# Another order of the first steps, and of attention's steps in the later batches, in a fused block attention and gated MLP kernel

## The chip, the cores and the metric

The kernel runs on one core of a Trainium2 chip. The metric is the device time of one launch in microseconds. The engines of the core work side by side, each through its own queue in order: TensorE (PE, matmuls), VectorE (DVE), ScalarE (ACT), GpSimd (POOL), and SyncE (SP), whose queue issues all DMAs here.

## What is computed

Eight batches of 576 tokens go through block attention (8 heads of 64, chunks of 64 tokens that attend only to themselves), and its result x through a gated MLP with a residual:

```python
scores = scale * np.matmul(q_c, k_c.transpose(0, 1, 2, 4, 3))       # per chunk and head, 64 x 64
attn = softmax(scores);  x = attn @ v_c                             # x: 8 x 576 x 512
h = gelu_tanh(x @ w_in)                                             # 512 -> 1024
u, v = h[..., :512], h[..., 512:]
v_n = (v - mean(v)) / np.sqrt(var(v) + 1e-06) * g_ln                # over the 512 columns
v_s = np.einsum('ts,bsd->btd', w_sg, v_n) + b_sg[None, :, None]     # mixes the 576 tokens
out = x + (u * v_s) @ w_out
```

All is float32. Matmuls split each operand into a high and a low part and add three products.

## The kernel before

**Attention** goes by 36 tiles of 128 rows (two chunks, all heads); a batch has 4.5. A tile takes three steps. `S` (att_scores): 16 matmuls of 64x64 into PSUM (from tile 5 on at L393), then softmax: maximum and subtraction on DVE (L404, L417), exp on ACT (L420), sum and reciprocal on DVE (L426 to L428), division on POOL (L429; on DVE up to tile 8). `T` (att_transpose): from tile 5 on a block transpose on DVE (L443), a copy on ACT (L446), two small copies on ACT (L451) and two on DVE (L453). `O` (att_out): 16 matmuls (L481) into a PSUM buffer, which ACT and DVE empty into xh, xl and xf, the high part, the low part and the whole of x (L101, L104, L503).

**The MLP** of a batch goes by units. `v0` to `v4` (v_unit, 12 matmuls of 512 columns, L523): gelu on ACT (L526), statistics on DVE, a power on POOL, normalization on DVE and ACT. An even batch has five (the fifth holds the odd 64 tokens of two batches, L545 to L547), an odd one four. `u0` to `u3` (24 matmuls of 288 columns, L560): gelu (L567). `s0` to `s3` (token mixing, 28 matmuls, L580): the product with u on DVE (L585), more sums, and its split into gh and gl. Then the output: batches 0 and 1 in four units `o` (24 matmuls, L700); later batches in seven products `p1 p5 p2 p6 p3 p7 p4` (12 matmuls each, L647) of quarter matrices, whose sums of w_out are formed once (`B`, ten POOL adds, L265), split (`C`, split_sum, L278) and kept in DRAM. `p4` runs after the next batch's v0 (the name `last`).

**Buffers** that tie steps together: three PSUM buffers `pm` for all units and for `O` (a unit waits until the one three before it has been emptied), one pair of banks for scores, 3 softmax tiles `pt`, 2 transposed tiles `ptT`.

**The order.** START is a hand-written list for the beginning: w_in's loads and conversion (L, W, w for the v half, X, x for the u half), attention's steps (A loads, S, T, O, and P and Q for S and O of two tiles), w_sg's split (G, g), w_out's conversion (Y), fill matmuls (D), and the units with batch and number (`s12` is s2 of batch 1). It ends within batch 2. From there a loop goes through the units of each batch in program order, and SLOTS says after which unit attention's steps for the coming tiles are recorded: the line 1 for odd batches, 0 for even ones, digits counting tiles from the first of that even batch or, in an odd batch, of the next even one. A step at p7 of an even batch comes only after the next batch's v0 (the list `later`). A scheduler orders what has been recorded; from batch 2 on PE's matmuls keep the written order, while DVE, ACT and POOL may take other orders.

Of the kernel before, what the change touches and what calls it, by code (L numbers as in the profile page):

```python
# [42 lines left out]


START = """
L0 A0 L1 A1 L2 L3 A4 W0 S0 W1 D8 w0 S1 W2 T0 w1 S2 O0 T1 W3 w2 S3 O1 T2 M0 w3 S4 O2 T3 v00 X0 O3 G0 T4 v01 x0 X1 O4 A8
v02 x1 X2 v03 X3 v04 u00 x2 g0 g1 u01 x3 g2 P5 g3 u02 g4 T5 u03 T6 s00 P7 Q5 s01 s02 T7 T8 s03 v10 Q7 v11 Y0 v12 Y1
v13 Y2 u10 Y3 u11 Y4 u12 Y5 Y6 u13 Y7 A10 s10 A12 s11 P9 s12 s13 T9 o00 B0 T10 P11 o01 B1 o02 B2 o03 Q9 B3 A14 T11 o10
B4 T12 o11 Q11 S13 A15 C5 B5 o12 B6 T13 o13 P14 A17 C6 B7 v20 B8 v21 O13 C7 B9 v22 K0
"""  # L50

PE_TILES = 5
# [5 lines left out]


SLOTS = {  # L60
    1: "v0:T0 v1:T1 u0:O01 u0:S23 u2:T2 u3:T3 s0:O23 s0:S4 p2:T4 p7:S56",
    0: "v0:O4 v3:T5 u0:T6 u1:O56 u1:S78 u3:T7 s0:T8 p7:O78 p7:S9A",
}


# [754 lines left out]
```

## Time and profile before

| | us |
|---|---|
| median of three runs (518.04 to 520.42) | 518.08 |
| the profiled execution, its own time | 519.43 |
| its span | 517.5 |
| PE busy in it | 491.1 |
| DVE, ACT, POOL busy | 385.6, 288.9, 90.8 |

A matmul's end in the trace is modelled, so that PE looks busy also where matmuls stand far apart. What a stage loses is read from the distance between the starts of its units, against the same units in a stretch without waits. TensorE's granted clock is 1.00 (2.4 GHz) almost everywhere and 0.50 (1.2 GHz) in two short stretches.

### The profile page before, as it was taken

The page shows a single profiled execution, that of the slowest core. Times are in us where ns is not written, and L with a number is a line of the kernel's source. Part 1 is how long each engine was busy: PE and PEld are TensorE (multiplying, and loading weights), DVE is VectorE, ACT ScalarE, POOL GpSimd, SP SyncE. Part 2 cuts the span into 40 slices and gives each one's busy share as a digit, 9 for nine tenths or more (in the row PEclk, how much of TensorE's full clock was granted, in tenths as well). Part 3 has the DMA queues.
Part 4 walks back from the last instruction along what each step waited for, and adds up shares of the span by engine and source line. Part 5 has one row for each costly group of instructions (what it writes and reads, how often), then busy time and mean ns, then how long its engine had stood idle before and what let it go on. Part 6 is the DMA issues. An engine that isn't in the chain of part 4 may idle for free.

```text
span 517.5 us, 12516 instructions
## 1 busy us (share of the span) xinstructions
PE 491.1 (95%) x5172; PEld 451.6 (87%) x5172; DVE 385.6 (75%) x783; ACT 288.9 (56%) x533; POOL 90.8 (18%) x94
## 2 busy tenths in 40 slices
PE   5999999999988969999999999999999999999996
PEld 4667898799987759997999889997899889998996
DVE  7998779988877856567869786667869786666165
ACT  5898767744264657217763678417763678414220
POOL 0112100202323601102120221102120221102000
PEclk9999999999999888999999999999999999999999
DMA  8857010245175784097444804087444910082006
GB/s 328 324 163 198 1 42 15 91 122 145 70 227 170 218 292 85 4 311 187 124 122 138 275 27 124 4 305 191 124 123 138 265 38 1 3 297 78 0 10 204
DMA packets 61356, 72.28 MB, mean 140 GB/s; under 512 B 36082, under 2 KB 47858, under 8 KB 61300
## 3 DMA queue, kind: packets, MB, share of 16 engines
q1 hardware_dynamic: 61300, 71.49, 45.1%
q8 instruction: 40, 0.66, 0.5%
q14 instruction: 16, 0.13, 0.1%
HBM read 58.36 MB, written 13.11 MB: 138 GB/s over the span
## 4 chain that ended last, share of the span: by engine, by line
PE 62%; DVE 20%; ACT 10%; POOL 2%; issue 2%; DMA 2%; SPq 0%; ACTq 0%; DVEq 0%; POOLq 0%
PE pm L580 17%; PE pm L560 14%; PE pm L523 14%; PE pm L647 9%; PE pm L700 3%; DVE xl L104 2%; PE banks L393 2%; DVE gl L104 2%; PE pm L185 1%; DVE sm L529 1%; DVE ptT L453 1%; DVE pt L417 1%; PE pm L481 1%; DVE v L541 1%; DVE den L426 1%
## 5 line engine op out<-in xcount | busy, mean ns | idle before, releaser
L580 PE MATMUL pm<-wsg,v 128*128 128x288 f32 x768 | 108.0, 297 | 0.5 <-ACT u L567 0.5
L580 PEld LDWEIGHTS pm<-wsg,v 128*128 128x128 f32 x768 | 103.9, 189 | 1.3 <-ACT u L567 1.0
L532 POOL TENSOR_TENSOR sm<-sm,neg_half 128x1 f32<-128x1 f32 x36 | 36.4, 1012 | 167.6 <-DVE sm L531 164.1
L523 PE MATMUL pm<-win_h,xl 128*128 128x512 f32 x128 | 52.3, 409 | 4.5 <-ACT hs L526 2.5
L560 PE MATMUL pm<-xh,win_l 128*128 128x288 f32 x256 | 56.3, 301 | 0.0
L429 POOL TENSOR_TENSOR pt<-pt,den 128x512 f32<-128x512 f32 x27 | 28.4, 1063 | 155.2 <-DVE den L428 134.3
L560 PE MATMUL pm<-xl,win_h 128*128 128x288 f32 x256 | 55.6, 299 | 0.0
L560 PE MATMUL pm<-xh,win_h 128*128 128x288 f32 x256 | 55.5, 298 | 0.0
L523 PE MATMUL pm<-win_l,xh 128*128 128x512 f32 x128 | 51.6, 403 | 0.0
L523 PE MATMUL pm<-win_h,xh 128*128 128x512 f32 x128 | 51.4, 401 | 0.0
L101 ACT CAST gh<-u 128x576 fp32r<-128x576 f32 x24 | 16.2, 675 | 50.5 <-DVE u L585 26.7
L560 PEld LDWEIGHTS pm<-xh,win_l 128*128 128x128 f32 x256 | 41.9, 191 | 1.3
L560 PEld LDWEIGHTS pm<-xh,win_h 128*128 128x128 f32 x256 | 41.6, 191 | 0.0
L560 PEld LDWEIGHTS pm<-xl,win_h 128*128 128x128 f32 x256 | 41.6, 191 | 0.0
L647 PE MATMUL pm<-gh,ring 128*128 128x288 f32 x192 | 40.1, 295 | 0.0
L540 ACT ACTIVATE v<-hs,sm 128x512 fp32r<-128x512 f32 x32 | 23.2, 725 | 24.6 <-POOL sm L532 24.6
L526 ACT ACTIVATE hs<-pm 128x512 f32<-128x512 f32 x36 | 21.1, 595 | 25.7 <-PE pm L523 25.4
L529 DVE BATCH_NORM_STATS2 sm<-hs 128x6 f32<-128x512 f32 x36 | 24.4, 684 | 14.1 <-ACT hs L526 14.1
L523 PEld LDWEIGHTS pm<-win_h,xl 128*128 128x128 f32 x128 | 24.4, 191 | 11.8 <-ACT hs L526 2.9
L647 PE MATMUL pm<-tv,ring 128*128 128x288 f32 x216 | 32.4, 299 | 1.8 <-ACT ptT L446 1.2
L541 DVE SCALAR_TENSOR_TENSOR v<-hs,sm,v 128x512 fp32r<-128x512 f32 x32 | 24.4, 762 | 11.3 <-ACT v L540 11.1
L104 DVE TENSOR_TENSOR gl<-u,gh 128x576 fp32r<-128x576 f32 x24 | 18.4, 765 | 18.9 <-ACT gh L101 18.9
(146 smaller groups left out, 1049.6 us busy)
## 6 DMA issues: line engine op xcount, KB each, us to landing
ring<-factors SPq DMA_DIRECT2D x42, 512.0 KB, 4.9
qkv_t<-qkv SPq DMA_DIRECT2D x32, 512.0 KB, 4.9
qkv_t<-qkv SPq DMA_DIRECT2D x124, 64.0 KB, 4.0
out_dram<-u SPq DMA_DIRECT2D x18, 288.0 KB, 4.9
out_dram<-ot SPq DMA_DIRECT2D x14, 288.0 KB, 3.7
qkv_t<-qkv SPq DMA_DIRECT2D x3, 768.0 KB, 11.8
wsg<-w_in SPq DMA_DIRECT2D x4, 512.0 KB, 6.2
wout<-w_in SPq DMA_DIRECT2D x4, 512.0 KB, 8.5
```

Source lines behind the costliest of these rows:

```text
L101: nc.scalar.copy(hi, src)
L104: lo_eng.tensor_tensor(lo, src, hi.bitcast(F32), op=ALU.subtract)
L429: (nc.gpsimd if t > last[1] else pick(f"n{t}")).tensor_tensor(pt, pt, den.unsqueeze(2).broadcast_to([P, H, D]), op=ALU.mult)
L523: pin(nc.tensor.matmul(pv, a[:, kt, tok], c[:, kt, DH:], start=(i == 0), stop=(i == 11)))
L526: nc.scalar.activation(h, pv, AF.Gelu_apprx_tanh, scale=-1.0)
L529: nc.vector.bn_stats(st, h)
L532: nc.gpsimd.tensor_tensor(rs, rs, neg_half, op=ALU.pow)
L540: nc.scalar.mul(hi, h, rs)
L541: nc.vector.scalar_tensor_tensor(lo, h, rs, hi.bitcast(F32), op0=ALU.mult, op1=ALU.subtract)
L560: pin(nc.tensor.matmul(pm[:, j, :HS], a[:, kt, dc], c[:, kt, j * HS : (j + 1) * HS], start=(i == 0), stop=(i == 11)))
L580: pin(nc.tensor.matmul(pm[:, j, :HS], a[:, dc], c[:, m, j * HS : (j + 1) * HS], start=(i == 0), stop=(i == len(ops) - 1)))
L647: pin(nc.tensor.matmul(pm[:, e, :HS], a[:, k, e * P : (e + 1) * P], c[:, k, :], start=starts and i == 0, stop=i == len(ops) - 1, skip_grou ...
```

## The change

Two tables of step names are replaced; no function changes, and every unit, tile and instruction form stays. Of START the first line and, below it, the part from batch 1's mixing units on (the conversion of w_out, Y, also moves ahead of more of batch 1's units, and v04 behind u00); SLOTS whole:

```diff
-L0 A0 L1 A1 L2 L3 A4 W0 S0 W1 D8 w0 S1 W2 T0 w1 S2 O0 T1 W3 w2 S3 O1 T2 M0 w3 S4 O2 T3 v00 X0 O3 G0 T4 v01 x0 X1 O4 A8
+L0 A0 L1 A1 L2 S0 D6 L3 W0 A4 W1 w0 S1 W2 w1 T0 S2 O0 T1 w2 W3 O1 T2 M0 w3 S3 O2 S4
...
-v13 Y2 u10 Y3 u11 Y4 u12 Y5 Y6 u13 Y7 A10 s10 A12 s11 P9 s12 s13 T9 o00 B0 T10 P11 o01 B1 o02 B2 o03 Q9 B3 A14 T11 o10
-B4 T12 o11 Q11 S13 A15 C5 B5 o12 B6 T13 o13 P14 A17 C6 B7 v20 B8 v21 O13 C7 B9 v22 K0
+s10 o00 A10 P9 A12 T9 s11 A14 s12 T10 s13 B0 P11 o01 B1 o02 B2 T11 B3 Q9 o03 A15 o10 B4 T12 B5 C5 o11
+B6 S13 Q11 o12 T13 B7 C6 o13 B8 A17 v20 O13 B9 C7 P14 v21 v22 K0
...
 SLOTS = {
-    1: "v0:T0 v1:T1 u0:O01 u0:S23 u2:T2 u3:T3 s0:O23 s0:S4 p2:T4 p7:S56",
-    0: "v0:O4 v3:T5 u0:T6 u1:O56 u1:S78 u3:T7 s0:T8 p7:O78 p7:S9A",
+    1: "v1:T1 v2:T0 u0:O01 u0:S23 u3:T3 u3:T2 s0:S4 s0:O23 p3:S56 p7:T4",
+    0: "v0:O4 u0:T6 u1:S78 u2:T5 s1:O56 s2:T8 s3:T7 p3:O78 p3:S9A",
 }
```

The line numbers of the kernel after are higher by one. Three places in the order of the engines' queues:

**ACT, batch 2, from the end of its v units into its u units**, before (`z` belongs to v4, `fac` is the split of a w_out sum, `u` the gelu of u0 and u1, `ptT` the transposes of tile 15, the next four rows empty the output of tiles 14 and 15):

```order
181 L545 ACTIVATE z_0_94<-hs,sm 64x512
182 L545 ACTIVATE z_1_95<-hs,sm 64x512
183 L546 CAST z_0_96<-z_0_94 64x512
184 L546 CAST z_1_97<-z_1_95 64x512
185 L277 CAST fac<-sums 128x512
186 L567 ACTIVATE u_2407<-pm 128x576 x2
187 L446 COPY ptT<-blocks 128x512
188 L451 COPY ptT<-blocks 32x8x32 x2
189 L101 CAST xh<-pm 128x2x4x64
190 L503 COPY xf<-pm 128x2x4x64
191 L101 CAST xh<-pm 128x2x4x64
192 L503 COPY xf<-pm 128x2x4x64
```

and after, the same stretch:

```order
187 L546 ACTIVATE z_0_94<-hs,sm 64x512
188 L546 ACTIVATE z_1_95<-hs,sm 64x512
189 L547 CAST z_0_96<-z_0_94 64x512
190 L547 CAST z_1_97<-z_1_95 64x512
191 L278 CAST fac<-sums 128x512
192 L568 ACTIVATE u_2397<-pm 128x576 x2
193 L447 COPY ptT<-blocks 128x512 x2
194 L452 COPY ptT<-blocks 32x8x32 x3
195 L421 ACT_TABLE_LOAD
196 L421 ACTIVATE pt<-pt 128x512 x2
197 L568 ACT_TABLE_LOAD
198 L568 ACTIVATE u_2397<-pm 128x576
```

Before, the output of tiles 14 and 15 (its emptying starts with `xh`) follows tile 15's copies directly; now the copies of both tiles are followed by the softmax of tiles 16 and 17 and the gelu of u2, and the emptying begins seven rows behind the last row shown. Ahead of the stretch, the exps of tiles 14 and 15 stood together before v20's gelu, with one table load behind them; now they stand apart among the gelus of v21 to v24, with four table loads.

**ACT, the first v units of batch 3**, before (`hs` is a gelu of a v unit, L420 the exp of tiles 18 and 19, L446 and L451 their transposes):

```order
206 L540 ACTIVATE v<-hs,sm 128x512
207 L420 ACT_TABLE_LOAD
208 L420 ACTIVATE pt<-pt 128x512 x2
209 L526 ACT_TABLE_LOAD
210 L526 ACTIVATE hs<-pm 128x512
211 L446 COPY ptT<-blocks 128x512 x2
212 L451 COPY ptT<-blocks 32x8x32 x4
213 L540 ACTIVATE v<-hs,sm 128x512
214 L526 ACTIVATE hs<-pm 128x512 x2
```

and after:

```order
218 L421 ACT_TABLE_LOAD
219 L421 ACTIVATE pt<-pt 128x512 x2
220 L527 ACT_TABLE_LOAD
221 L527 ACTIVATE hs<-pm 128x512
222 L541 ACTIVATE v<-hs,sm 128x512
223 L527 ACTIVATE hs<-pm 128x512
224 L447 COPY ptT<-blocks 128x512
225 L452 COPY ptT<-blocks 32x8x32 x2
226 L527 ACTIVATE hs<-pm 128x512
227 L541 ACTIVATE v<-hs,sm 128x512
228 L447 COPY ptT<-blocks 128x512
229 L452 COPY ptT<-blocks 32x8x32 x2
```

The exp now comes ahead of v0's gelu, and each tile's copies stand a v unit further back, between gelus.

**DVE, the products of batch 3**, before (`kept`, `ot` and `u` by L653 empty the products, `tv` is the split for p7 and p4, L443 the block transpose of tile 22):

```order
414 L653 TENSOR_TENSOR kept<-pm,xf 128x576
415 L653 TENSOR_TENSOR ot<-pm,kept 128x576
416 L104 TENSOR_TENSOR tv<-u_3104,tv 128x576
417 L443 STREAM_TRANSPOSE blocks<-pt 128x512
418 L653 TENSOR_TENSOR u_3104<-pm,xf 128x2x288
419 L453 COPY ptT<-blocks 32x8x32 x2
420 L653 TENSOR_TENSOR u_3104<-pm,u_3104 128x2x288
```

and after:

```order
419 L654 TENSOR_TENSOR kept<-pm,xf 128x576
420 L654 TENSOR_TENSOR ot<-pm,kept 128x576
421 L105 TENSOR_TENSOR tv<-u_3102,tv 128x576
422 L654 TENSOR_TENSOR u_3102<-pm,xf 128x2x288
423 L444 STREAM_TRANSPOSE blocks<-pt 128x512
424 L654 TENSOR_TENSOR u_3102<-pm,u_3102 128x2x288
425 L454 COPY ptT<-blocks 32x8x32 x2
```

The block transpose has gone from ahead of p6's sum (`u<-pm,xf`) to behind it.

## Rows read from the trace of the kernel before

**Rows 1.** Page, parts 1 and 6: busy us and share; a load's KB, us to landing.

```profile
PE 491.1 (95%) x5172; PEld 451.6 (87%) x5172; DVE 385.6 (75%) x783; ACT 288.9 (56%) x533; POOL 90.8 (18%) x94
...
qkv_t<-qkv SPq DMA_DIRECT2D x32, 512.0 KB, 4.9
```

**Rows 2.** Stages: us, busy PE, PEld, DVE, ACT, POOL (count), clock, DMA share, GB/s.

```profile
0.00:66.90 66.90, 59.53 (x616) 46.07 (x617) 57.97 (x124) 52.27 (x127) 9.91 (x14) 1.00 0.60 196
66.90:145.35 78.45, 77.54 (x874) 73.60 (x873) 66.66 (x153) 43.95 (x85) 15.81 (x13) 1.00 0.31 90
145.35:202.14 56.79, 47.90 (x550) 43.03 (x549) 41.02 (x81) 32.84 (x58) 16.15 (x16) 0.91 0.71 212
...
226.62:286.00 59.38, 57.13 (x694) 53.22 (x692) 44.84 (x90) 35.26 (x58) 10.31 (x11) 1.00 0.57 168
286.00:343.11 57.11, 57.11 (x578) 53.74 (x577) 43.06 (x86) 33.66 (x55) 10.54 (x11) 1.00 0.40 123
```

**Rows 3.** Chain that ended last: start us, us, engine, tile, line, matmul passes.

```profile
194.45 7.86 PE pm L560 x48
...
292.58 11.20 PE pm L523 x48
303.78 6.40 PE pm L560 x48
310.18 1.09 PE pm L481 x64
...
318.79 14.91 PE pm L580 x112
333.71 9.56 PE pm L647 x72
```

**Rows 4.** PE's timeline, 145 to 203 us: start us, us, line, [idle before <-releaser].

```profile
149.16 0.79 PE L481 MATMUL pm<-ptT,qkv_t 64*64 64x64 f32 x32 [0.45 <-ACT xf L503]
150.91 1.05 PE L481 MATMUL pm<-ptT,qkv_t 64*64 64x64 f32 x29 [0.96 <-ACT ptT L451]
...
169.06 0.50 PE L523 MATMUL pm<-win_h,xl 128*128 128x512 f32 x1 [2.48 <-ACT hs L526]
...
191.19 1.44 PE L481 MATMUL pm<-ptT,qkv_t 64*64 64x64 f32 x29 [4.90 <-ACT ptT L451]
```

**Rows 5.** The two stretches at the lower clock (the ninth field).

```profile
169.95:173.35 3.40, 3.40 (x10) 2.62 (x9) 3.40 (x9) 2.34 (x6) 3.27 (x4) 0.50 1.04 290
...
190.45:197.25 6.80, 6.06 (x108) 5.80 (x109) 3.23 (x7) 3.98 (x8) 0.00 (x0) 0.50 1.02 272
```

**Rows 6.** ACT's timeline, 184 to 200 us.

```profile
184.83 1.47 ACT L545 ACTIVATE z<-hs,sm 64x512 fp32r<-64x512 f32 x2 [2.32 <-POOL sm L532]
...
190.74 0.83 ACT L451 COPY ptT<-blocks 32x256 f32<-32x256 f32 x2
...
196.57 1.28 ACT L420 ACT_TABLE_LOAD   x1
197.87 1.38 ACT L420 ACTIVATE pt<-pt 128x512 f32<-128x512 f32 x2
```

**Rows 7.** PE's timeline in batch 3: two rows with a wait.

```profile
246.53 1.16 PE L481 MATMUL pm<-ptT,qkv_t 64*64 64x64 f32 x64 [1.35 <-ACT hs L526]
...
284.25 1.82 PE L647 MATMUL pm<-tv,ring 128*128 128x288 f32 x12 [0.62 <-ACT ptT L446]
```

**Rows 8.** DVE's timeline ahead of these two waits.

```profile
240.53 0.71 DVE L443 STREAM_TRANSPOSE blocks<-pt 128x512 f32<-128x512 f32 x1 [1.09 <-POOL pt L429]
...
282.81 0.70 DVE L443 STREAM_TRANSPOSE blocks<-pt 128x512 f32<-128x512 f32 x1
```

**Rows 9.** DVE's and POOL's timelines, 142 to 152 us.

```profile
143.19 2.44 DVE L453 COPY ptT<-blocks 32x256 f32<-32x256 f32 x2 [0.74 <-ACT ptT L446]
...
150.46 0.60 DVE L453 COPY ptT<-blocks 32x256 f32<-32x256 f32 x2 [0.68 <-ACT ptT L446]
...
142.83 2.66 POOL L265 TENSOR_TENSOR sums<-sums,wout 128x512 f32<-128x512 f32 x2
```

More of the change, by code (lines that the diff above doesn't have):

```diff
@@ L45 @@
 START = """
-L0 A0 L1 A1 L2 L3 A4 W0 S0 W1 D8 w0 S1 W2 T0 w1 S2 O0 T1 W3 w2 S3 O1 T2 M0 w3 S4 O2 T3 v00 X0 O3 G0 T4 v01 x0 X1 O4 A8
-v02 x1 X2 v03 X3 v04 u00 x2 g0 g1 u01 x3 g2 P5 g3 u02 g4 T5 u03 T6 s00 P7 Q5 s01 s02 T7 T8 s03 v10 Q7 v11 Y0 v12 Y1
-v13 Y2 u10 Y3 u11 Y4 u12 Y5 Y6 u13 Y7 A10 s10 A12 s11 P9 s12 s13 T9 o00 B0 T10 P11 o01 B1 o02 B2 o03 Q9 B3 A14 T11 o10
-B4 T12 o11 Q11 S13 A15 C5 B5 o12 B6 T13 o13 P14 A17 C6 B7 v20 B8 v21 O13 C7 B9 v22 K0
+L0 A0 L1 A1 L2 S0 D6 L3 W0 A4 W1 w0 S1 W2 w1 T0 S2 O0 T1 w2 W3 O1 T2 M0 w3 S3 O2 S4
+T3 X0 v00 O3 T4 x0 X1 v01 X2 v02 O4 x1 x2 A8 X3 v03 G0 u00 g0 g1 P5 x3 T5 g2 v04 u01 g3 u02
+g4 u03 T6 s00 P7 Q5 s01 s02 T7 T8 s03 v10 Y0 Y1 Y2 Q7 v11 v12 u10 Y3 u11 v13 Y4 u12 u13 Y5 Y6 Y7
+s10 o00 A10 P9 A12 T9 s11 A14 s12 T10 s13 B0 P11 o01 B1 o02 B2 T11 B3 Q9 o03 A15 o10 B4 T12 B5 C5 o11
+B6 S13 Q11 o12 T13 B7 C6 o13 B8 A17 v20 O13 B9 C7 P14 v21 v22 K0
 """
```

## The prediction

> **What bounds the kernel now.** The page's first part [rows 1] names PE: busy 95% of the span. Since a modelled end makes PE look busy, I next cut the span into stages [rows 2] and took the price of a unit from the piece of the chain where PE runs through without a wait [rows 3]: four v units 11.20 us (2.80 each), two u units 6.40 (3.20), four s units 14.91, six products 9.56 (1.59), two tiles of attention's O 1.09. An o unit has the matmuls of a u unit, so 3.20; S has those of O, so 1.09 for two tiles. Each stage is then its clean sum and an excess.
>
> - Even batch 4, from 286.00: S of two tiles 1.09, five v 14.00, O of one tile 0.55, p4 1.59, four u 12.80, O and S of two tiles 2.18, s 14.91, products 9.56: 56.68, measured 57.11 [rows 2]. Excess 0.4, a tenth for each switch between kinds of work. This is PE at its bound.
> - Odd batch 3, from 226.62: v 11.20, p4 1.59, u 12.80, s 14.91, products 9.56, three O of two tiles 3.27, S of five tiles 2.73: 56.06, measured 59.38. Excess 3.3.
> - The end of batch 1 and the head of batch 2, 145.35 to 202.14: three o units 9.60, five v 14.00, four u 12.80, O and S of five tiles each 5.46: 41.86, measured 56.79. Excess 14.9.
> - 66.90 to 145.35: PE is busy 77.54 of 78.45, so little is to be had.
> - 0 to 66.90: DVE is busy 57.97, about as long as PE (59.53). This stage is set by conversions on DVE and ACT more than by PE.
>
> The 14.9 has four places. PE waits 0.45 and 0.96 for the O of tiles 11 and 12, 2.48 for a PSUM buffer at v22, and 4.90 for the O of tiles 14 and 15 [rows 4]. After the last two of these the granted clock stands at 0.50, the 1.2 GHz level, for 3.40 and 6.80 us [rows 5]; PE has little work in the first part of the second stretch, so this costs half of the first, 1.7, and the 1.46 by which u22 and u23 exceed two clean units (7.86 against 6.40) [rows 3]. That makes 12.0; the rest is the pipeline running empty and full at each wait, and switches.
>
> **The change, part by part.**
>
> *Batch 2, the O of tiles 14 and 15.* Before, ACT reaches the copies of tile 15 after v24's z work, which begins at 184.83 after a wait for POOL, and the split of a w_out sum; it ends the last at 191.57 [rows 6], while PE asks at the end of u21. The change leaves the copies there but asks later: S of two tiles 1.09, u22 and u23 6.40, s20 and s21 7.46 come first, 14.9 us. Against that stand the old 4.9 and what now precedes the copies on ACT: the softmax of tiles 14 and 15 falls between v21 and v24, with four more table loads of 1.28 [rows 6], 5.1 us. Some 4.9 us are left over. The wait goes, and with it the second stretch at 1.2 GHz. What is late next there is the gelu of u20 and u22: ACT has so much behind v23 that I count 0 to 1 us of waiting for a PSUM buffer at u23 or s21.
>
> *v22.* Its buffer was v20's, whose gelu stood behind the exps of tiles 14 and 15. The new START has v20, O13, then those scores, and the gelu goes first. The 2.48 and the first stretch at 1.2 GHz go.
>
> *Tiles 11 and 12.* T12 now has o11 and S13, 3.75 us, between o10's end and its O; its chain is o10's sum and the block transpose on DVE, 0.70 each [rows 8], and ACT's copy and small copies, at most 0.83 each [rows 6]: 3.1. It just fits. Against it speaks [rows 9]: two small DVE copies took 2.44 where the same took 0.60 later, while POOL formed sums of w_out (142.83 to 145.49). The change starts these sums earlier, next to the transposes of tiles 11 to 13. I take 0.5 as the new wait, with 0 to 2 as bounds.
>
> The Trainium skill has the rule for this (SBUF — State Buffer, "Who interferes with whom"): DVE copies in a two-port mode and GpSimd share one port pair, and the second to start is blocked to the first's end. The 2.44 agrees. Where every such copy hits a sum, the stage would come out as in the first rival.
>
> So 13.9 of the 14.9 can go (1.0 stays for ten switches), less 0.9 of new waits: **13.0**.
>
> *Odd batches 3 and 5.* Before, S of the next two tiles comes after v0 and their T directly behind. DVE stands before the block transpose until POOL has divided (1.09) [rows 8], v units' statistics queue behind it, gelus are late, and O waits 1.35 for a buffer [rows 7]; later T of tile 22 stands on DVE ahead of p6's sum (0.70 at 282.81), and p7 waits 0.62. After, S comes ahead of p7, and p7, v0, p4 and v1 (8.8 us) lie before the first T, v2, v3 and u0 (8.8 us) between it and O. DVE's transpose of tile 22 stands behind p6's sum, and S of two tiles covers p7. Two table loads go per odd batch. Batch 5 repeats batch 3. From the excess of 3.3 I leave 0.5 for switches: 2.8 each, 5.6. New: O in front of p7 needs its PSUM buffer a product earlier, v1 of the next even batch may wait for v0's gelu behind two exps and a table load, and in batch 2 the O of tiles 14 and 15 at s21 puts DVE behind for p2: 0 to 0.5 in five places, taken as 0.6. So **5.0**.
>
> *SP's queue.* In even batches the loads of two tiles now stand ahead of p7's ring load and store. The ring place is read a batch later, and the store must be out only before the gelu of the next u0, over 14 us on. Without that cover it would be a landing, 4.9 [rows 1]. I take nothing.
>
> *The first 145 us.* The same instructions in another order, against DVE that is full. PE could gain little: its 7.4 idle us lie for the most part before the first tile has landed. S0 ahead of W0, two fill passes less and v04 behind u00 can shift three or four us either way: I take **0**, with -3 to +3 as bounds. w_out's conversion, which now moves ahead of s10, has DVE 85% busy beside it [rows 2]; if it delays o00, up to 2.
>
> Sum: 13.0 + 5.0 + 0 = 18.0. Against the profiled execution's 519.43 that is 501.4; the median of the runs shown, 518.08, lies 1.35 lower, so **500.1**.
>
> **The rivals.**
> 1. The sums collide with the transposes of tiles 11 to 13. Each collision costs 2.44 less 0.60, 1.84; three of them on the path are 5.5 us: 505.6. For it: the one case in the trace. Against it: between T11 and its O lie three o units.
> 2. ACT falls behind at v21 to v24 by its seven table loads, where three were. If a switch costs an engine drain beyond the 1.28, by as much again, the four more cost 5.1 further, the gelu of u22 misses s21, and a wait like the old one returns with its slow clock: 5.1 + 1.5, 506.7. Against it: the exp starts 1.30 after its load started, without a gap [rows 6]. The Trainium skill (ScalarE: Activation LUTs, "What ACT_TABLE_LOAD costs") gives 1.28 for the load, which agrees, and about 1.38 more for a drain, which no row here shows.
> 3. The start gains too, since v00 to v03 no longer stand behind all u conversions: 3 us more, 497.
> 4. Nothing changes: DVE, not PE, sets the pace and the waits move. In the stage of 14.9 DVE is busy 41 of 56.79, so it does not: 518.
> 5. Slower: T runs late in every place where only one or two units cover it (O of tiles 2 and 3 in odd batches has s0 and S4, 4.3 us, behind T). From the point where DVE reaches the transposes more than 4.3 late, each O costs what that of 14 and 15 cost: 4.90 + 1.46 and 0.7 of running empty, 7.1. Three of them give back 21.3 of the 18.0: 521.4. Against it: already before, T3 has only s0 between itself and that O, and batch 3's waits lie elsewhere [rows 7].
>
> **How the numbers follow.** The forecast 0.61 (497 to 503.5), rival 1 0.13, rival 2 0.07, rival 3 0.08, a mix of partial gains between 508 and 515 0.03, rival 4 0.04, rival 5 0.04. A measurement tells 0.5%, 2.6 us, from no change. Only rivals 4 and 5 are not faster by that: faster 0.92, same 0.04, slower 0.04. The range takes in rivals 1 to 3 and the start's bounds: 495.5 to 508.
>
> **What would show it.** Right: no PE wait over 1 us from 145 us to the end but the last ring load; clock 1.00 throughout; v0 of batch 3 to v0 of batch 5 in 113.7 instead of 116.5 us; batch 1's last o unit to s20 in 43 to 44. Wrong: a wait at s21 for `ACT u`, at the O of tiles 11 and 12 for `ACT ptT`, p7 or v1 waiting in batches 3 to 5, or s00 starting more than 3 us from 66.9.

## The result, and the profile after

The changed kernel takes 502.36 us (four runs, 501.71 to 502.96) against 518.61 of the kernel before (four runs, 518.04 to 520.42): a ratio of 0.9681, 95% interval 0.9652 to 0.971. Predicted were 500.1, in a range of 495.5 to 508. The profiled execution took 502.69 us; its span is 500.9, where before it was 517.5. Line numbers in it are higher by one. One execution of all those measured, of the kernel with the O of tiles 14 and 15 at u3 (below), took 2673 us, with 17.79 us for a u unit of 3.20 while the granted clock read 1.00; its cause is open, and no number here rests on it.

The first and the second part of the page of after, the row of all engines and that of TensorE's clock in 40 slices:

```profile
PE 486.7 (97%) x5168; PEld 448.6 (90%) x5168; DVE 381.9 (76%) x783; ACT 289.4 (58%) x533; POOL 92.5 (18%) x94
...
PEclk9999999999999999999999999999999999999999
```

PE is busy 4.4 us less than in [rows 1] with the same matmuls: that is about what the two stretches at 1.2 GHz had added. Both stretches of [rows 5] are gone: the clock is 1.00 up to PE's last matmul.

After's stages, cut where the same units start (columns as in [rows 2]: length, busy time of PE, PEld, DVE, ACT, POOL, granted clock, DMA share, GB/s):

```profile
67.39:145.97 78.58, 77.47 (x874) 73.60 (x873) 66.39 (x153) 46.00 (x89) 16.46 (x14) 1.00 0.33 93
145.97:187.16 41.19, 41.19 (x487) 37.66 (x486) 33.50 (x69) 30.75 (x50) 13.79 (x13) 1.00 0.76 248
187.16:216.48 29.32, 28.83 (x379) 27.64 (x377) 21.52 (x41) 15.50 (x27) 3.75 (x4) 1.00 0.50 146
216.48:272.42 55.94, 55.84 (x630) 52.70 (x629) 44.93 (x90) 34.06 (x55) 10.58 (x11) 1.00 0.59 169
272.42:330.88 58.46, 58.46 (x642) 54.70 (x641) 43.30 (x88) 32.75 (x56) 10.52 (x11) 1.00 0.41 126
```

To compare them, a step that changed its stage has to be counted with it. The second stage lost the O of tiles 14 and 15 (1.09): 56.79 less 1.09 is 55.70, now 41.19, a gain of 14.5. The third gained that O and the O and S ahead of p7 (0.98 and 1.04): 29.32 less 3.11 is 26.2, where before it was 24.48, a loss of 1.7. The first lost 0.1. Batches 3 and 4 together (the last two rows) are 114.40 us, 116.49 before: a gain of 2.1. Batches 5 and 6 take 113.49; they hold 1.04 us less of such work than before, so their gain is 2.0. Batch 7 and the end give 0.4, and the first mixing unit starts 0.5 later. The sum, 16.6, is the difference of the spans.

Where the old waits stood, PE's timeline of after shows none (the O of tiles 11 and 12, then that of 14 and 15); the third row is ACT's last copy for tile 15:

```profile
149.78 1.14 PE L482 MATMUL pm<-ptT,qkv_t 64*64 64x64 f32 x64
194.70 1.16 PE L482 MATMUL pm<-ptT,qkv_t 64*64 64x64 f32 x64
...
190.69 0.40 ACT L452 COPY ptT<-blocks 32x256 f32<-32x256 f32 x1
```

The copy ends at 191.09, 3.6 us before PE asks. Behind 67 us PE still loses 1.4 us at batch 1's v2 (1.2 before), 0.45 at the last ring load (0.53 before), and more than a few tenths in two other places, those of these rows: an early product p2 of batch 2 that waits for a split of g on DVE, and in batches 3 and 5 the O of tiles 2 and 3, which takes 1.51 us instead of 1.09 since ACT's small copies for it end while it runs:

```profile
207.92 0.40 PE L648 MATMUL pm<-gl,ring 128*128 128x288 f32 x1 [0.43 <-DVE gl L105]
...
248.79 1.58 PE L482 MATMUL pm<-ptT,qkv_t 64*64 64x64 f32 x64
...
247.49 1.67 ACT L452 COPY ptT<-blocks 32x256 f32<-32x256 f32 x4
```

### The profile page after: what moved, and what is told of

It reads as the page before. It is cut to its first block, busy times and chain, and to the rows that moved or that the text cites. A ratio compares the mean times of both kernels' runs of the same rounds, so it can differ in the third digit from the quotient of the medians.

```text
span 500.9 us, 12504 instructions
## 1 busy us (share of the span) xinstructions
PE 486.7 (97%) x5168; PEld 448.6 (90%) x5168; DVE 381.9 (76%) x783; ACT 289.4 (58%) x533; POOL 92.5 (18%) x94
## 4 chain that ended last, share of the span: by engine, by line
PE 53%; DVE 20%; ACT 14%; POOL 5%; DMA 3%; issue 3%; SPq 1%; POOLq 0%; ACTq 0%; DVEq 0%
PE pm L581 17%; PE pm L648 11%; PE pm L561 10%; PE pm L524 9%; POOL sm L533 3%; DMA qkv_t<-qkv 2%; DVE den L427 2%; PE pm L482 2%; DVE xl L105 2%; ACT v L541 2%; DVE blocks L444 2%; DVE sm L530 2%; DVE v L542 2%; POOL pt L430 1%; ACT ptT L447 1%
## 5 line engine op out<-in xcount | busy, mean ns | idle before, releaser
L533 POOL TENSOR_TENSOR sm<-sm,neg_half 128x1 f32<-128x1 f32 x36 | 38.4, 1069 | 149.1 <-DVE sm L532 141.5
L102 ACT CAST gh<-u 128x576 fp32r<-128x576 f32 x24 | 16.2, 675 | 45.1 <-POOL u L605 24.4
L648 PEld LDWEIGHTS pm<-gh,ring 128*128 128x128 f32 x192 | 31.4, 188 | 0.3 <-ACT xf L504 0.2
L447 ACT COPY ptT<-blocks 128x512 f32<-128x512 f32 x31 | 19.0, 619 | 21.7 <-DVE blocks L444 16.9
L586 DVE TENSOR_TENSOR u<-pm,u 128x576 f32<-128x576 f32 x24 | 18.1, 754 | 17.4 <-PE pm L581 17.0
```

Source lines behind the costliest of these rows:

```text
L102: nc.scalar.copy(hi, src)
L447: nc.scalar.copy(ptT, blocks)
L533: nc.gpsimd.tensor_tensor(rs, rs, neg_half, op=ALU.pow)
L586: nc.vector.tensor_tensor(g, pm[:, :, :HS], g, op=ALU.mult)
L648: pin(nc.tensor.matmul(pm[:, e, :HS], a[:, k, e * P : (e + 1) * P], c[:, k, :], start=starts and i == 0, stop=i == len(ops) - 1, skip_grou ...
```

## The experiments

Each kernel differs from the kernel after in the two tables alone. Losses are read from unit starts, as in the prediction. Beside these runs the kernel before had medians of 518.7 to 519.0 us; the kernel after, run again in the last experiment, has a median of 502.6 over its eight runs.

### Each table alone

START of before with SLOTS of after:

```diff
 START = """
-L0 A0 L1 A1 L2 S0 D6 L3 W0 A4 W1 w0 S1 W2 w1 T0 S2 O0 T1 w2 W3 O1 T2 M0 w3 S3 O2 S4
+L0 A0 L1 A1 L2 L3 A4 W0 S0 W1 D8 w0 S1 W2 T0 w1 S2 O0 T1 W3 w2 S3 O1 T2 M0 w3 S4 O2 T3 v00 X0 O3 G0 T4 v01 x0 X1 O4 A8
...
```

> SLOTS of after with START of before: the loop's places alone. Theory (each place has its own wait, and the gains add): the wait of 4.90 us at the O of tiles 14 and 15 goes with its slow clock (1.46) and the running empty (0.7), 7.1 us, and the odd batches give 4.1, as in after; v22's 2.48 with its slow clock and the 0.45 and 0.96 at tiles 11 and 12 stay: 518.6 - 11.2 = 507.4 us. Rival (the two tables need one another: with the exps of tiles 14 and 15 together ahead of the gelu of v20, ACT is late for everything up to s21): part of the 7.1 comes back as a wait at u22, u23 or s21, 510 to 514 us.

Measured: 508.06 us (507.81 to 508.31). START of after with SLOTS of before, the other half:

```diff
-    1: "v1:T1 v2:T0 u0:O01 u0:S23 u3:T3 u3:T2 s0:S4 s0:O23 p3:S56 p7:T4",
-    0: "v0:O4 u0:T6 u1:S78 u2:T5 s1:O56 s2:T8 s3:T7 p3:O78 p3:S9A",
+    1: "v0:T0 v1:T1 u0:O01 u0:S23 u2:T2 u3:T3 s0:O23 s0:S4 p2:T4 p7:S56",
+    0: "v0:O4 v3:T5 u0:T6 u1:O56 u1:S78 u3:T7 s0:T8 p7:O78 p7:S9A",
```

> START of after with SLOTS of before: the written list alone. Theory (gains add): the waits at v22 and at the O of tiles 11 and 12 go with the first slow stretch, 5.6 us, less 0.5 for the later s00; the wait at the O of tiles 14 and 15 stays near 4.9, the odd batches stay as before: 518.6 - 5.1 = 513.5 us. Rival (ACT sets the time of tile 15's copies, whatever PE does): PE comes to that O 5 us earlier and waits 5 us longer, about 10 in all, and the total stays at 517 to 518.6 us.

Measured: 515.08 us (514.3 to 515.53). In the first kernel the timeline of PE shows the wait at the O of tiles 11 and 12 and the one at v22 unchanged to 0.01 us, the latter followed by the lower clock (third row, by stretch):

```profile
150.92 1.05 PE L481 MATMUL pm<-ptT,qkv_t 64*64 64x64 f32 x29 [0.96 <-ACT ptT L451]
169.06 0.50 PE L523 MATMUL pm<-win_h,xl 128*128 128x512 f32 x1 [2.47 <-ACT hs L526]
...
169.50:173.00 3.50, 3.50 (x10) 2.69 (x9) 3.50 (x10) 2.44 (x7) 3.36 (x3) 0.53 1.01 293
```

In the second, PE's timeline, a stretch of PE's clock and ACT's timeline at the O of tiles 14 and 15:

```profile
186.42 1.45 PE L482 MATMUL pm<-ptT,qkv_t 64*64 64x64 f32 x29 [6.71 <-ACT ptT L452]
...
186.00:190.00 4.00, 3.58 (x97) 3.32 (x98) 1.23 (x3) 1.98 (x5) 0.00 (x0) 0.50 0.52 114
...
185.97 0.83 ACT L452 COPY ptT<-blocks 32x256 f32<-32x256 f32 x2
```

SLOTS alone behaves as the theory has it (508.1 for 507.4). START alone falls between theory and rival: PE comes to that O 6.6 us earlier than before (179.02 against 185.59), ACT's copies end only 4.8 us earlier (186.80 against 191.57), and the wait grows from 4.90 to 6.71. So the two gains, 10.6 and 3.6, do not add to the 16.2 of the whole change: 2 us come only when both waits go, for what START gains ahead of the O is partly waited away there.

### The line for odd batches

```diff
-    1: "v1:T1 v2:T0 u0:O01 u0:S23 u3:T3 u3:T2 s0:S4 s0:O23 p3:S56 p7:T4",
+    1: "v0:T0 v1:T1 u0:O01 u0:S23 u2:T2 u3:T3 s0:O23 s0:S4 p2:T4 p7:S56",
```

> After with the line of SLOTS for odd batches as before; the line for even batches and START as after. Theory (the odd line alone makes the gain of batches 3 and 5): 502.4 + 4.1 = 506.5 us, v0 of batch 3 to v0 of batch 5 in about 116.5 us. Rival (part of it came from the even line, whose T, S and O ahead of p7 leave ACT and DVE freer at the head of the odd batch): 504.5 us or less, and 115.5 us or less from v0 to v0.

Measured: 504.08 us (503.35 to 504.69), and 115.19 us from v0 of batch 3 to v0 of batch 5. The theory falls: the odd line is worth 1.7 us in all. The other 2.4 of the gain in the odd batches belong to the line for even batches, whose last entries now put the O and S of the next tiles ahead of p7 and not behind the odd batch's v0. With that alone the wait of 1.35 in [rows 7] is gone; its 0.62 at p7 stays, as PE's timeline of batch 3 shows in this kernel, beside a wait at s0 for the gelu of a u unit:

```profile
243.31 3.45 PE L581 MATMUL pm<-wsg,v 128*128 128x288 f32 x24 [0.23 <-ACT u L568]
268.88 1.83 PE L648 MATMUL pm<-tv,ring 128*128 128x288 f32 x12 [0.63 <-ACT ptT L447]
```

### The head of START

The steps up to s03 as before (the first diff of this section goes on to `s03` in the same way), those from `v10` on as after.

> After with the part of START up to s03 as before; all behind it as after. Theory (the new head costs 0.5 us and nothing behind it takes this up): s00 starts at 66.9 instead of 67.4 us, total 501.9 us. Rival (the 0.5 is given back by the wait at batch 1's first v units, 1.2 to 1.4 us in both kernels, which DVE sets): 502.4 us, with a longer wait at v12.

Measured: 502.08 us (501.65 to 502.33); s00 starts at 67.28, and v12 loses 1.2 us, as in the kernel before (1.4 in after). Neither theory nor rival: the old head starts s00 no earlier here, and the wait at v12 is not longer. Over all profiles of this study the new head has s00 at 66.0 to 67.9 us (nine profiles, mean 67.02), the old one at 66.87 to 67.28 (four, mean 66.99). Up to s00 the heads differ by nothing that these runs can show, and the 0.5 us of the first comparison was the scatter of one profile.

### The cover of the O of tiles 14 and 15

```diff
-    0: "v0:O4 u0:T6 u1:S78 u2:T5 s1:O56 s2:T8 s3:T7 p3:O78 p3:S9A",
+    0: "v0:O4 u0:T6 u1:S78 u2:T5 u3:O56 s2:T8 s3:T7 p3:O78 p3:S9A",
```

> After with the O of tiles 14 and 15 (even batches: tiles 5 and 6 of the pair) recorded behind u3 instead of s1, 7.5 us earlier on PE; the transposes as in after. Theory (cover is plain time: tile 15's copies end on ACT at 191.09 us, behind the exps of tiles 16 and 17, and this O would be asked for at 187.2): PE waits about 3.9 us in batch 2, and with the running empty and a stretch at the lower clock this costs 4.5 to 6: 507 to 508.5 us. Rival (the scheduler takes the copies ahead of the exps once the O is recorded earlier, and they end by 187): no wait, 502.4 us.

Measured: 506.1 us (505.93 to 506.9, three runs). The trace is from a further run of the same kernel.

> The O of tiles 14 and 15 behind u3 once more, for a trace (the first one's profiled execution took 2673 us, its three others 505.9 to 506.9). Theory (cover is plain time): a wait of about 3.9 us between 187 and 191 us, released by ACT's small copies of tile 15, and some slow clock behind it: 506 us. Rival: the 4 us are lost elsewhere, by later gelus of u2 and u3 behind the emptying of that O on ACT, with waits at s20 to s23.

Measured: 507.52 us (one run). PE's timeline, two stretches of its clock, and ACT's last copy for tile 15:

```profile
190.75 1.98 PE L482 MATMUL pm<-ptT,qkv_t 64*64 64x64 f32 x62 [3.96 <-ACT ptT L452]
192.66 5.23 PE L581 MATMUL pm<-wsg,v 128*128 128x288 f32 x24
...
187.00:191.00 4.00, 0.25 (x8) 0.25 (x12) 2.05 (x8) 3.92 (x7) 1.08 (x2) 0.85 0.00 2
191.00:193.00 2.00, 2.00 (x63) 1.88 (x60) 1.00 (x2) 0.55 (x2) 0.97 (x1) 0.50 0.11 20
...
190.29 0.40 ACT L452 COPY ptT<-blocks 32x256 f32<-32x256 f32 x1
```

The theory holds: PE asks at 186.5 us, ACT ends its copies at 190.69, about where they ended in after, and the difference is waited, 3.96 for the 3.9 expected. The wait costs more than itself: the O takes 6.19 instead of 1.09, and s20 behind it 5.60 instead of 3.72, at a clock that is 0.50 from 191 on. Some 1.5 of these 7 us come back up to batch 3, where the wait at p2 does not appear; the medians show 3.5 to 5.

### The scores of tiles 14 and 15 ahead of v20

First in front of o13, one unit too early:

```diff
-B6 S13 Q11 o12 T13 B7 C6 o13 B8 A17 v20 O13 B9 C7 P14 v21 v22 K0
+B6 S13 Q11 o12 T13 P14 B7 C6 o13 B8 A17 v20 O13 B9 C7 v21 v22 K0
```

> After with the scores of tiles 14 and 15 (P14) back ahead of v20, so that both exps stand together and ahead of v20's gelu on ACT, with four table loads fewer up to v24. Theory (that order made v22's wait): PE waits 2.5 us at v22, and the stretch at the lower clock costs 1.7 more: 506.5 us. Rival (v22 waited because of the later O of tile 13, or because of T12, not because of the exps; then the four table loads saved are worth something or nothing): no wait at v22, 501.5 to 502.4 us.

Measured: 506.62 us (505.66 to 507.57), as the theory says and for another reason. PE's timeline has no wait at v22, but one between the scores of tile 14 and those of tile 15, for a load (the second row is the stretch behind it, with the clock):

```profile
157.28 0.69 PE L394 MATMUL banks<-qkv_t 64*64 64x64 f32 x32 [2.22 <-DMA qkv_t<-qkv]
...
158.00:163.00 5.00, 5.00 (x26) 4.95 (x27) 4.32 (x10) 2.34 (x6) 0.44 (x1) 0.66 0.69 191
```

The load of a tile needs one of four buffers, and the O of an earlier tile frees it. This run said nothing on v22; the time alone would have passed for a proof.

Then directly behind o13, where P14 stands in the kernel before:

```diff
-B6 S13 Q11 o12 T13 B7 C6 o13 B8 A17 v20 O13 B9 C7 P14 v21 v22 K0
+B6 S13 Q11 o12 T13 B7 C6 o13 P14 B8 A17 v20 O13 B9 C7 v21 v22 K0
```

> After with P14 directly behind o13, where it stands in the kernel before; the run with P14 one unit further ahead, in front of o13, stood at a load (2.2 us) and told nothing of v22. The exp of tile 14 now stands ahead of v20's gelu on ACT, that of tile 15 behind it. Theory (the exps ahead of that gelu made v22's wait): PE waits 1 to 2.5 us at v22 and up to 1.7 more go with the lower clock: 504 to 506.5 us. Rival (the wait needs the late O of tile 13 of the kernel before as well, or other work on ACT): no wait at v22, 502 us.

Measured: 506.75 us (506.33 to 507.18). PE's timeline (the unit behind v22), its clock, and ACT's timeline:

```profile
170.95 0.50 PE L524 MATMUL pm<-win_h,xl 128*128 128x512 f32 x1 [2.43 <-ACT xf L504]
...
171.00:175.00 4.00, 4.00 (x12) 3.19 (x13) 2.02 (x4) 3.10 (x5) 2.51 (x2) 0.67 0.60 210
...
162.67 0.63 ACT L421 ACTIVATE pt<-pt 128x512 f32<-128x512 f32 x1 [2.75 <-DVE pt L418]
163.32 1.28 ACT L527 ACT_TABLE_LOAD   x1
164.61 0.60 ACT L527 ACTIVATE hs<-pm 128x512 f32<-128x512 f32 x1
...
170.53 0.37 ACT L504 COPY xf<-pm 128x256 f32<-128x256 f32 x1
```

ACT stands 2.75 us before the exp of tile 14, whose input DVE has not made yet; the gelu of v20 and the emptying of tile 13's O stand behind it, the table loads and the exp of tile 15. The kernel before has the same picture on ACT, ahead of the gelus whose first one frees v22's buffer:

```profile
163.98 0.63 ACT L420 ACTIVATE pt<-pt 128x512 f32<-128x512 f32 x1 [2.93 <-DVE pt L417]
165.96 0.63 ACT L420 ACTIVATE pt<-pt 128x512 f32<-128x512 f32 x1 [1.35 <-DVE pt L417]
...
168.41 1.09 ACT L526 ACTIVATE hs<-pm 128x512 f32<-128x512 f32 x2
```

The exps are short (0.63 each); ACT's standing before them until DVE has made their input, and the table load behind them, hold the queue as well. So, in the run with P14 behind o13, the wait is of the old size (2.43 against 2.48 in [rows 4]) and the clock falls behind it as it did, but it comes one unit later and for the buffer of tile 13's O, since that O now stands ahead of v21. That these scores, one unit earlier, cost such a wait is shown by this run, and v22's wait behind the exps is read from the rows of before. At v22 itself PE does not wait here, which is what the rival said: which buffer is the late one depends on the order around it.

### The O of tiles 11 and 12 without cover

```diff
-s10 o00 A10 P9 A12 T9 s11 A14 s12 T10 s13 B0 P11 o01 B1 o02 B2 T11 B3 Q9 o03 A15 o10 B4 T12 B5 C5 o11
-B6 S13 Q11 o12 T13 B7 C6 o13 B8 A17 v20 O13 B9 C7 P14 v21 v22 K0
+s10 o00 A10 P9 A12 T9 s11 A14 s12 T10 s13 B0 P11 o01 B1 o02 B2 T11 B3 Q9 o03 A15 o10 B4 T12 B5 C5 Q11 o11
+B6 S13 o12 T13 B7 C6 o13 B8 A17 v20 O13 B9 C7 P14 v21 v22 K0
```

> After with the O of tiles 11 and 12 ahead of o11 instead of behind o11 and the scores of tile 13, so that nothing lies between T12 and it. Theory: it is asked for at 146.0 us, its last copies on DVE end at 149.2; PE waits 3.2 us, and 1 to 2 more go with the running empty and the lower clock: 506 to 508 us. Rival 1 of the prediction in its place (these copies meet a sum of w_out on POOL, as the ones of tile 11 at 141.14, 1.98 us instead of 0.60): 1.4 us more, 508 to 509.

Measured: 505.31 us (504.99 to 505.84). No wait of 3 us appears. Ahead of batch 2 the scheduler may mix PE's matmuls, and it puts about half of o11 between the O of tile 11 and that of tile 12 and mixes the rest with the latter; PE's timeline has 0.46 there and 1.15 at u20, for the gelu of a v unit on ACT (there the exp of tile 14 has come ahead of v21's gelu, which in after goes first):

```profile
146.46 0.53 PE L701 MATMUL pm<-gh,wout 128*128 128x288 f32 x2 [0.46 <-ACT xf L504]
...
175.28 0.53 PE L561 MATMUL pm<-xh,win_l 128*128 128x288 f32 x2 [1.15 <-ACT hs L527]
```

So the expected total was nearly met by other means: 3.2 us more up to s20, of which 1.5 by the mixing with its gaps at the O and 1.3 at u20. The rival's collision with POOL's sums does not come at tile 12, whose copies on DVE take 0.60 after POOL's sum has ended at 147.33. It comes at tile 13, whose copies take 1.65 beside other sums:

```profile
147.75 0.60 DVE L454 COPY ptT<-blocks 32x256 f32<-32x256 f32 x2 [0.69 <-ACT ptT L447]
...
158.21 1.65 DVE L454 COPY ptT<-blocks 32x256 f32<-32x256 f32 x2 [0.69 <-ACT ptT L447]
...
144.81 2.52 POOL L266 TENSOR_TENSOR sums<-wout 128x512 f32<-128x512 f32 x2
...
158.10 1.29 POOL L266 TENSOR_TENSOR sums<-wout,sums 128x512 f32<-128x512 f32 x1
```

### Two tries to remove what is left

The first, with the old head of START:

```diff
-    1: "v1:T1 v2:T0 u0:O01 u0:S23 u3:T3 u3:T2 s0:S4 s0:O23 p3:S56 p7:T4",
-    0: "v0:O4 u0:T6 u1:S78 u2:T5 s1:O56 s2:T8 s3:T7 p3:O78 p3:S9A",
+    1: "v1:T1 v2:T0 u0:O01 u0:S23 u3:T3 u3:T2 s0:S4 s1:O23 p3:S56 p7:T4",
+    0: "v0:O4 u0:T6 u1:S78 u2:T5 s1:O56 s3:T8 p1:T7 p3:O78 p3:S9A",
```

> START as in the run with the old head; in odd batches the O of tiles 2 and 3 goes behind s1 instead of s0; in even batches T of tile 8 goes behind s3 and T of tile 7 behind p1. Theory (the waits left in after are transposes and splits too close to their use): the 0.14 + 0.42 at that O goes in two batches, and the 0.90 at batch 2's p2 with 0.17 and 0.19 beside it: 502.1 - 2.3 = 499.8 us. Rival (p2, p6 and p3, 4.8 us, are too little for the chain behind T of tile 7): the O of tiles 7 and 8 ahead of p7 waits 2 to 5 us in three even batches, 508 us or more.

Measured: 502.89 us (501.99 to 505.28). The odd line gives its 0.28 in each of two batches. Batch 2's wait at `gl` is gone, and PE's timeline has others in its place: one for DVE's emptying (`kept`) in batch 2 and one ahead of the O of tiles 7 and 8 in batch 4, which loses 0.4 more than in after:

```profile
209.70 0.40 PE L649 MATMUL pm<-gh,ring 128*128 128x288 f32 x1 [0.43 <-DVE kept L655]
...
326.36 1.16 PE L483 MATMUL pm<-ptT,qkv_t 64*64 64x64 f32 x64 [0.29 <-DVE ot L655]
```

The second, with the line for odd batches as in the first:

```diff
-    0: "v0:O4 u0:T6 u1:S78 u2:T5 s1:O56 s2:T8 s3:T7 p3:O78 p3:S9A",
+    0: "v0:O4 u0:T6 u1:S78 u2:T5 s0:O56 s2:T8 s3:T7 p3:O78 p3:S9A",
```

> After with the O of tiles 14 and 15 behind s0 instead of s1 (even line) and the O of tiles 2 and 3 behind s1 instead of s0 (odd line). Theory: batch 2's p2 waits because DVE does the emptying of that O between s2 and the products without an idle moment from 200.8 us on; a unit earlier it falls where DVE idles (1.6 and 0.6 us at 194 and 198 us), its copies just fit (191.1 against 190.9); that gives up to 1.2 us, and the odd line 0.28 in each of two batches as in the run with more cover: 500.6 us. Rival (what is taken from one wait comes back at the next, as when T of tile 7 went later): 502 us, with 0.4 to 1 us of waits in batches 2, 4 and 6 somewhere from s0 to p7.

Measured: 502.01 us (501.89 to 502.25). With the O of tiles 14 and 15 a unit earlier, p2 loses 0.2; instead that O takes 1.51 (its copies end while it runs) and s23 waits for a buffer that ACT empties late. PE's timeline:

```profile
190.60 1.58 PE L482 MATMUL pm<-ptT,qkv_t 64*64 64x64 f32 x64
200.32 3.46 PE L581 MATMUL pm<-wsg,v 128*128 128x288 f32 x24 [0.50 <-ACT xf L504]
```

Beside it the kernel after, unchanged:

> The kernel after, unchanged, beside the one above on the same chip. Theory: 502.4 us within 0.5, and a start of s00 that differs from one profile to the next by up to a microsecond, since the same START gave 66.0, 66.5, 66.9, 67.4 and 67.6 in five profiles. Rival (the head's 0.5 us of the first comparison is a cost of the new head): s00 at 67.4 again.

Measured: 502.78 us (501.51 to 503.06), s00 at 67.41. That is the value which the rival named, but the other profiles with this head lie on both sides of it, from 66.0 to 67.9. The second try and after have the ratios 0.9678 (0.9663 to 0.9692) and 0.9687 (0.9668 to 0.9706) to the kernel before: no version here is faster than after by what can be measured. In the first try neither theory nor rival holds for the even line: the O ahead of p7 has a gap of 0.3 where the rival said 2 to 5. In the second the rival holds for batch 2; batch 4 has no new wait. In both, from s0 to p7 of batch 2, the wait taken away in one place came back in the next.

## Why the prediction came out as it did

The forecast was faster by 18.0; the profiles show 16.6, the medians 16.2. By its steps:

- **What bounds the kernel.** Right: PE, unit by unit. The clean sums held to 0.4 us: the stage from batch 1's last three o units to s20 has a clean sum of 41.86 less the moved O of 1.09, 40.8, and takes 41.19, less than the 43 to 44 named as its sign.
- **O of tiles 14 and 15.** Right in its cause; the size of the cover was 1.3 us too high. Predicted were 4.9 us left, measured 3.6. One reading was off: the last of the small copies does not stay ahead of the softmax of tiles 16 and 17, it comes behind their exps and the gelu of u22 (190.69; the other three start at 184.98). There is no wait at u23 or s21 for a gelu. The run with this O at u3 bears the step out: cover is plain time on ACT.
- **v22.** Right: the wait is gone, and P14 put back brings a wait of the old size, though for another buffer. The step named the exps; the rows of before show ACT standing ahead of them for DVE too, 1.35 us before the second one, which itself takes 0.63.
- **Tiles 11 and 12.** The 0.5 of new waiting did not come. The collision did, in a place where it costs nothing. DVE's and POOL's timelines of after:

```profile
141.14 1.98 DVE L454 COPY ptT<-blocks 32x256 f32<-32x256 f32 x2 [0.74 <-ACT ptT L447]
...
148.61 0.60 DVE L454 COPY ptT<-blocks 32x256 f32<-32x256 f32 x2 [0.69 <-ACT ptT L447]
...
140.30 1.30 POOL L266 TENSOR_TENSOR sums<-wout 128x512 f32<-128x512 f32 x1
141.68 1.28 POOL L266 TENSOR_TENSOR sums<-sums 128x512 f32<-128x512 f32 x1
```

  The copies of tile 11 took 1.98 while POOL formed two sums and ended with the second of them, near 143; tile 12's came after a sum and took 0.60. Rival 1 needed three of these on the path; there was one, off it. Its "one case in the trace" was a miscount, though: before had a second, of tile 13, with its copies at 1.50 beside POOL's sums:

```profile
160.23 1.50 DVE L453 COPY ptT<-blocks 32x256 f32<-32x256 f32 x2 [0.69 <-ACT ptT L446]
...
158.76 2.52 POOL L265 TENSOR_TENSOR sums<-wout 128x512 f32<-128x512 f32 x2
```

  These copies stand on DVE ahead of the work that the exp of tile 14 waited for. In after tile 13's take 0.78, in the run with P14 behind o13 they take 0.60 and the wait comes all the same.

  The Trainium skill's rule of the shared port pair (SBUF — State Buffer, "Who interferes with whom") fits the 1.98 as it fitted the 2.44.
- **The stage of 13.0.** 14.5 were gained up to s20, where the stage of the forecast ends, and 1.7 given back from s20 to the next v0. That their sum, 12.8, is so near to 13.0 is luck: two errors stand against each other. I had counted 1.0 us for switches and 0.9 for waits where 0.4 was left. And the wait of p2 in batch 2, named as one of five places at 0 to 0.5, cost 0.9, and 0.4 more in its neighbours. DVE's timeline shows why: from 200.00 on, where it empties the moved O, it idles 0.8 in 7 us up to the split of g that p2 waits for (207.11):

```profile
201.06 0.58 DVE L454 COPY ptT<-blocks 32x256 f32<-32x256 f32 x2 [0.37 <-ACT ptT L447]
202.04 0.69 DVE L105 TENSOR_TENSOR xl<-pm,xh 128x512 fp32r<-128x512 f32 x1 [0.39 <-ACT xh L102]
...
207.11 0.75 DVE L105 TENSOR_TENSOR gl<-u,gh 128x576 fp32r<-128x576 f32 x1
```

- **Odd batches, 5.0.** Measured 4.1. The term that was too small is that of new waits: the O of tiles 2 and 3 with the S ahead of it loses 0.14 and 0.42 in each of the two batches, where I had put the risk into rival 5 and nothing into the sum. p7 and v1 do not wait. Batch 4 gives a little back: it is 0.7 above its clean sum, 0.4 before. From v0 of batch 3 to v0 of batch 5 the sign was 113.7; it is 114.40. And the step did not say which line of SLOTS does what: 2.4 us come from the even line (O and S ahead of p7), which alone ends the wait of 1.35, and 1.7 from the odd line.
- **The first 145 us, 0.** Right: the heads do not differ in the mean of the profiles. The later o00 that w_out's conversion might have caused did not come (the stage from s00 is 0.1 longer).
- **Base.** I took 1.35 us between the profiled execution and the median. Later runs moved before's median up to 518.6 and more, and after's profiled execution lies 0.33 above its median. This is 1.0 of the 2.3 by which the forecast is too low, the odd batches 0.9, the start's scatter and the rest 0.4: a term as large as those argued over, and it was read from three runs.
- **Rival 2** falls by ACT's timeline of after, in the stretch with the most switches:

```profile
168.00 1.28 ACT L527 ACT_TABLE_LOAD   x1
169.30 0.60 ACT L527 ACTIVATE hs<-pm 128x512 f32<-128x512 f32 x1
169.91 1.28 ACT L421 ACT_TABLE_LOAD   x1
171.21 0.63 ACT L421 ACTIVATE pt<-pt 128x512 f32<-128x512 f32 x1
```

  Each function begins 1.30 us after its load begins, and a load 0.61 after the function before it, whose own time is 0.60: a switch costs 1.3 us here and nothing beside it.

  The Trainium skill (ScalarE: Activation LUTs, "What ACT_TABLE_LOAD costs") gives about 1.38 us more for a drain; the four rows leave no room for it.
- **Rivals 3 to 5** did not happen. The place of rival 5 was a real one, though: 0.56 us in each odd batch there, far from the 7.1 at which it would decide.

## What to carry to other kernels

A step that asks for another engine's result has a cover, the time between what starts the chain and the asking, and it can be worked out from one profile to a microsecond or so: put the asking behind that time and no further. Where the in-order queue of a helper engine holds work for two consumers, look at what stands ahead of the nearer one, a waiting instruction most of all. And when a stage has had its waits removed, expect the next limit within a microsecond: here four edits went at the waits left over; three moved them, one took 0.28 us out of batches 3 and 5 each, and none gave a time that could be measured.

## What the runs showed of the hardware

A long wait of PE within the work cost more than its length. In three kernels with one large wait added, of 2.22, 2.43 and 3.96 us, the stretch up to s20 grew by 4.3, 4.6 and 5.3 us (the last with the O that moved into it taken off), in part since the granted clock fell to 0.50, the 1.2 GHz level, during it or behind it: the rows above show 0.66, 0.67 and 0.50 as means of stretches of 5, 4 and 2 us, and in the third kernel s20 took 5.60 for 3.72. Behind the wait of 1.15 at u20, that of 1.35 in [rows 7] and those of 0.43 at p2 the clock stayed at 1.00.
